# New order for batches 0 to 2 of a planned attention and gated-MLP kernel

## The chip, the cores and the metric

The kernel runs on one core of one Trainium2 chip. A core has TensorE (PE, with the weight load PEld beside it), VectorE (DVE), ScalarE (ACT), GpSimd (POOL) and SyncE (SP), which here only issues DMAs, all in one queue. The metric is the device time of one execution in microseconds (us), as the median of several runs.

## The reference

Eight batches of attention (8 heads, 576 positions, 64 columns a head), whose output is the input of a gated MLP with a product over positions:

```
scores = q @ k.T / 8                     # per batch and head
heads 0-3: keep 0 <= i - j < 32          # local
heads 4-7: keep j <= i, i % 32 == j % 32 # strided
x  = softmax(scores) @ v                 # 8 x 576 x 512
h  = relu(x @ w_in)                      # 512 -> 1024
u, v = h[..., :512], h[..., 512:]
v_n = (v - mean(v)) / sqrt(var(v) + 1e-6)
v_s = w_spatial @ v_n + b_spatial[:, None]   # over the 576 positions
out = (u * v_s) @ w_out                  # 512 -> 512
```

All of it is fp32.

## The kernel before

**Precision.** An fp32 operand of the MLP is split into two parts of a shorter type: `rnd` (L419, recorded at L427 or L429) casts it to the high part, `rest` (L433, recorded at L437) subtracts that from the value to get the low part. Each product then takes three matmuls (high-high, high-low, low-high). So behind every operand of TensorE stand two small operations of ACT, DVE or POOL.

**Stages of a batch b.** Heads are worked in four pairs, t = 4b + hp, hp 0 and 1 local, hp 2 and 3 strided. Local scores are the products L565 and their output L675; strided scores L711 and their output L781; the result is split into x. Then come the value product (L1034, over four 128-wide slabs kt of x), its statistics and normalisation (`chain`, L992 to L1017), which gives vn; the gate product U (L1234); the spatial product (L1331, weights wsp_sb, 48 matmuls for four blocks of 128 columns; the last 64 positions, called the tail, and the bias come in at L1343 and L1344); the gating on DVE (L1354); and the output product (L1435), which is done as seven block products of half size on sums and differences of the blocks of g and of w_out (the sums are `combine`, L902). The w_in, wsp and w_out operands are brought in during the first batch: w_in and w_out come as pairs of words that ACT (L866), POOL or DVE (L875) and DVE (L883) put together, and are split like any operand.

**What sets the order.** Nothing is issued in the order of the code. Each operation is added to a `Program` with a key and with the engines that may do it and their assumed costs. `order` replays the program with those costs, and each engine that comes free takes the ready operation of lowest key. If an operation may run on DVE or POOL, it is given to whichever the replay ends first on, and DVE's end is made later for the comparison by a constant: `dp` holds one for operations with a single input and one for those with two, and they hold while the replay's clock is under `dpt`, else the constant is 0 (L293). The instructions are then written to each engine in this order, loads to SP. `KEYS` holds the keys: `a` for each of the first eight attention tiles, `v`, `u`, `s`, `t`, `o` for the slabs of w_in (value half, gate half), wsp, its tail and w_out, `lq`, `lw`, `lv`, `lu`, `lo`, `ls` for their loads, `cst`, `fill` and `set` for constants and clears, and `p`, `b`, `p2`, `b2`, `cl`, `ta`, `la`, `su`, `tu` for offsets in later stages. `fillers` (L332) puts matmuls on zeros (L1622) ahead of a product where the replay shows a gap: `w` holds until when in the replay, from which gap on, and for which share of it.

Of the kernel before, what the change touches and what calls it, by code (L numbers as in the profile page):

```python
# [39 lines left out]
TAIL = S - 4 * P  # L40
NT = 4
KEYS = {
    "a": (-7906.0, -7964.0, -15830.5, -4267.6, 1379.5, 702.2, 2039.1, -3334.8,),
    "v": (5971.0, -3908.5, -3534.4, 726.2,),
    "u": (4329.4, -8322.8, -3410.6, -6121.6,),
    "s": (13308.3, 1709.1, 5210.5, 13961.2,),
    "t": (2702.5,),
    "o": (1519.5, 3986.0, -8051.8, 12581.5,),
    "cst": (-11921.6,),
    "lead": (-1.3,),  # L50
    "fill": (-7688.6, 5328.4, -10489.4, 9430.7, 11172.9, 3859.6,),
    "dp": (12894.8, -1038.4,),
    "dpt": (657.16,),
    "lv": (-2858.0, -4582.1, -8989.4, -1041.3,),
    "lu": (66.6, -1740.1, -5229.0, 1297.1,),
    "lo": (-7685.9, 12601.4, 4211.2, 6006.6,),
    "ls": (3541.9, 11770.0, 12130.5, 1637.8, 8461.5,),
    "near": (4868.39,),
# [4 lines left out]
    "set": (-100.0, -90.0, -90.0,),  # L63
    "w": (110.0, 0.7, 0.8,),
    "p2": (11.39, 28.77, 1.25,),
    "b2": (-94.81, -0.95, -162.68, -62.31, 5.91, 7.53, 69.31, -30.15, -133.03, -14.06, 0.12,),
    "cl": (-13.99, 175.03, -54.21, -178.21, -336.22, -30.36,),
    "ta": (482.31, 200.01,),
    "la": (8.82, -81.27, -24.66, -78.03,),
    "su": (240.79, 97.41,),  # L70
    "tu": (-0.95, -65.62, 102.01, 7.87, 89.32, -152.34, 100.98, -246.45,),
}
U_COST = 11.2
WARM_COST, WARM_COLS = 427.0, 256
PE_MASKED, APART = (0, 1, 2, 3), (0, 1)
OTHER_BANK = (1, 2, 3)
# [87 lines left out]
class Program:  # L164
# [39 lines left out]
    def order(self):  # L204
# [41 lines left out]
        while len(issued) < len(ops):  # L246
# [14 lines left out]
            now, e = best  # L261
# [28 lines left out]
                cost += FETCH_COST * max(0.0, -stock)  # L290
            now = max(free[e], ready_at[n][e])
            locks = POOL in self.port.get(n, ()) and self.share[n] == 1
            held = KEYS["dp"][locks] if now < KEYS["dpt"][0] * 1000.0 else 0.0  # L293
            other = []
            for o, c in ops[n][1]:
                if o != e:
# [2 lines left out]
            if other and min(other)[0] < now + cost + shared(n, e, now, cost)[0] + held * (e == DVE):  # L299
                e = min(other)[1]  # L300
                cost = dict(ops[n][1])[e]
                now = max(free[e], ready_at[n][e])
            taken[n] = True
            if e in self.port.get(n, ()):
                more, theirs = shared(n, e, now, cost)
                cost += more
                p = peer[e]
# [55 lines left out]
def attention_moe(ctx, tc, qT, kT, ks, vl, vs, cst, eye, w_in, w_out, wsp, wtail, out):  # L363
# [839 lines left out]
    def moe_1(b, key):  # L1203
        if b >= SEVEN:
            moe_u(b, key)
            key += U_COST
        vn = vns[b] = r_vn.new()
# [499 lines left out]
```

## Time and profile before

| what | value |
|---|---|
| median of 3 runs | 516.87 us (516.08 to 517.52) |
| the profiled execution | 518.85 us |
| its span on the core | 517.0 us, 14639 instructions |
| mean granted TensorE clock | 0.979 |
| traffic | 42.27 MB read, 9.44 MB written, 100 GB/s over the span |
| loads, KB each: q, k, kbd, v_raw (local), xt or v_raw (strided) | 295, 304, 144, 384, 512 |
| loads, KB each: one slab of w_in or w_out, cst, eye | 512, 96, 64 |

The span is what the core's trace covers; the execution's own time holds 1.85 us more. In the rows, "x" stands for x0 and x1, "m", "po" and "s" are accumulation tiles, "pts" and "ptl" the transposed attention weights; a row of a timeline is a start, a length, the engine, the line and what is written from what, with the idle time ahead of it and what ended that in brackets.

### The profile page before, as it was taken

What the parts mean: (1) busy time and instruction counts of PE and PEld (TensorE: products, weight loads), DVE (VectorE), ACT (ScalarE), POOL (GpSimd) and SP (SyncE); (2) the same over time, 40 slices, a digit from 0 to 9 for tenths busy, and PEclk for the clock granted to TensorE, in tenths of its full rate; (3) what the DMA queues carried; (4) which work ended last, traced back from release to release, by engine and by line L of the source; (5) the groups of instructions that cost most, each with busy time, mean ns of one, the idle gap of its engine ahead of it and who ended that gap; (6) DMA issues with size and microseconds to landing.
All of it is one profiled execution on the core that took longest, in us unless ns stands there. A gap on an engine that the chain in (4) does not pass through costs nothing.

```text
span 517.0 us, 14639 instructions
## 1 busy us (share of the span) xinstructions
PE 494.2 (96%) x5824; PEld 451.1 (87%) x5824; DVE 407.8 (79%) x1140; ACT 270.9 (52%) x801; POOL 142.3 (28%) x256
## 2 busy tenths in 40 slices
PE   6779979999999999899999999999999998999997
PEld 4558879989899899899899998999899997899897
DVE  2799899969489769998699958997699648784566
ACT  5786765569453685476354646457264414241222
POOL 3455864043222134211131306212120102210200
PEclk9688989999999999999999999999999999999999
DMA  8796522444035413233033603324030300011002
GB/s 273 296 335 231 182 83 81 168 123 135 2 125 159 144 49 115 93 112 109 2 119 113 195 2 94 115 67 129 1 97 20 115 1 2 1 46 47 1 1 93
DMA packets 26244, 52.65 MB, mean 102 GB/s; under 512 B 3136, under 2 KB 11584, under 8 KB 26176
## 3 DMA queue, kind: packets, MB, share of 16 engines
q1 hardware_dynamic: 26176, 51.72, 30.1%
q8 instruction: 46, 0.75, 0.6%
q14 instruction: 22, 0.18, 0.1%
HBM read 42.27 MB, written 9.44 MB: 100 GB/s over the span
## 4 chain that ended last, share of the span: by engine, by line
PE 79%; DVE 10%; DMA 4%; POOL 2%; ACT 2%; issue 1%; SPq 1%; POOLq 0%; DVEq 0%; ACTq 0%
PE m L1034 17%; PE m L1331 17%; PE m L1435 15%; PE m L1157 10%; PE m L1234 5%; PE po L781 4%; PE po L675 3%; PE s L565 2%; PE m L1343 2%; DMA outT<-vv 2%; PE s L711 1%; DVE x L437 1%; DVE vn L437 1%; PE m L1344 1%; DMA k<-kT 1%
## 5 line engine op out<-in xcount | busy, mean ns | idle before, releaser
L1331 PE MATMUL m<-wsp_sb,vn 128*128 128x288 f32 x720 | 106.4, 299 | 5.3 <-DVE wsp_sb L437 3.8
L1331 PEld LDWEIGHTS m<-wsp_sb,vn 128*128 128x128 f32 x720 | 100.1, 191 | 7.4 <-DVE wsp_sb L437 4.1
L1034 PE MATMUL m<-w_in_sb,x 128*128 128x512 f32 (+1 forms) x408 | 100.9, 403 | 0.0
L1034 PEld LDWEIGHTS m<-w_in_sb,x 128*128 128x128 f32 (+1 forms) x408 | 75.5, 188 | 19.4 <-DVE x L437 0.2
L992 ACT ACTIVATE vv<-m 128x512 f32<-128x512 f32 (+1 forms) x37 | 21.8, 596 | 65.8 <-PE m L1034 65.3
L429 POOL TENSOR_SCALAR ptl<-pc 32x320 f32<-32x320 f32 (+3 forms) x86 | 41.5, 483 | 53.1 <-PE po L675 18.8
L1435 PE MATMUL m<-g,w_out_sb 128*128 128x288 f32 x384 | 55.5, 296 | 0.0
L622 ACT ACTIVATE pl<-pl,ml 128x64 f32<-128x64 f32 (+1 forms) x140 | 47.2, 341 | 15.3 <-DVE ml L602 15.1
L1010 POOL TENSOR_TENSOR bn<-bn,sel 128x1 f32<-128x1 f32 (+1 forms) x37 | 21.8, 593 | 115.1 <-DVE bn L1005 114.1
L1435 PEld LDWEIGHTS m<-g,w_out_sb 128*128 128x128 f32 x384 | 52.4, 188 | 0.3 <-DVE o L1463 0.2
L1435 PE MATMUL m<-vn,w_out_sb 128*128 128x288 f32 x288 | 42.1, 297 | 0.0
L997 DVE BATCH_NORM_STATS2 bn<-vv 128x6 f32<-128x512 f32 (+1 forms) x37 | 25.4, 686 | 19.8 <-ACT vv L992 19.5
L429 POOL TENSOR_SCALAR pts<-pc 32x288 f32<-32x288 f32 x37 | 17.5, 472 | 84.8 <-DVE pc L765 59.1
L1234 PE MATMUL m<-x,w_in_sb 128*128 128x288 f32 x288 | 40.2, 297 | 0.0
L1435 PEld LDWEIGHTS m<-vn,w_out_sb 128*128 128x128 f32 x288 | 39.2, 188 | 0.7 <-DVE o L1463 0.2
L427 ACT COPY ptl<-pc 32x64 f32<-32x64 f32 (+3 forms) x106 | 36.4, 345 | 6.0 <-DVE pc L646 3.1
L1234 PEld LDWEIGHTS m<-x,w_in_sb 128*128 128x128 f32 x288 | 38.8, 188 | 0.7
L1017 DVE TENSOR_SCALAR vv<-vv,bn 128x512 f32<-128x512 f32 (+1 forms) x37 | 21.2, 572 | 13.9 <-POOL bn L1010 13.7
L427 ACT CAST g<-u 128x576 fp32r<-128x576 f32 (+1 forms) x33 | 20.0, 610 | 19.2 <-DVE u L1356 12.7
L1168 DVE TENSOR_TENSOR u<-m,vv 128x288 f32<-128x288 f32 x30 | 13.4, 449 | 18.7 <-PE m L1157 18.6
L622 ACT ACTIVATION_READ_ACCUMULATOR pl<-pl,ml 128x1 f32 (+1 forms) x140 | 26.8, 191 | 0.0
L437 DVE TENSOR_TENSOR g<-u,g 128x576 fp32r<-128x576 f32 (+1 forms) x40 | 24.5, 631 | 0.8 <-ACT g L427 0.7
(187 smaller groups left out, 967.1 us busy)
## 6 DMA issues: line engine op xcount, KB each, us to landing
q<-qT SPq DMA_DIRECT2D x30, 295.0 KB, 4.2
outT<-o SPq DMA_DIRECT2D x48, 144.0 KB, 1.8
k<-kT SPq DMA_DIRECT2D x16, 304.0 KB, 4.3
kbd<-ks SPq DMA_DIRECT2D x32, 144.0 KB, 3.6
v_raw<-vl SPq DMA_DIRECT2D x11, 384.0 KB, 5.0
v_raw<-vs SPq DMA_DIRECT2D x8, 512.0 KB, 5.1
xt<-vs SPq DMA_DIRECT2D x7, 512.0 KB, 3.6
outT<-vv SPq DMA_DIRECT2D x16, 144.0 KB, 1.8
```

The costliest lines, as they stand in the source:

```text
L427: eng.copy(dst(), src())
L429: eng.tensor_scalar(dst(), src(), 1.0, 0.0, op0=ALU.mult, op1=ALU.add)
L437: eng.tensor_tensor(dst(), src(), f32(hi()), op=ALU.subtract)
L622: eng.activation(p_sb()[:m, u, :], src, AF.Exp, bias=st()[:m, u : u + 1], scale=SCALE if masked else -1.0, **total,)
L992: lambda eng: eng.activation(v()[:m], v_ps()[:m, :], AF.Relu), [(v_ps,)], [(v,)],
L997: lambda eng: eng.bn_stats(bn()[:m, 0:6], v()[:m]), [(v,)], [(bn,)],
L1010: lambda eng: eng.tensor_tensor(bn()[:m, 9:10], bn()[:m, 8:9], sel[:m, 0:1], op=ALU.pow),
L1034: eng.matmul(v_ps()[:m, :], x_at(kt)[:, a, :], w_in_sb[:, w, kt, HF:], start=(n == 0 and i == 0), stop=(n == NT - 1 and i == 2),)
L1157: eng.matmul(o_ps()[:, :HS], w_at(w)[:, a * P : (a + 1) * P], x_at(j), start=first and kk == 0 and i == 0, stop=kk == 1 and i == 2, skip_g ...
L1234: eng.matmul(u_ps()[:, :HS], w_in_sb[:, w, kt, f * P : (f + 1) * P], xs[NHP * b + kt]()[:, a, r], start=(n == 0 and i == 0), stop=(n == NT ...
L1331: eng.matmul(s_ps()[:, :HS], vn()[:, a, kt, fs], wsp_sb[:, w, kt, r], start=(kt == 0 and i == 0), stop=False,)
L1435: eng.matmul(o_ps()[:, :HS], w_out_sb()[:, b_at, w, kk, a * P : (a + 1) * P], at(j, kk), start=first and kk == 0 and i == 0, stop=kk == 1 ...
```

## The change

New values for nearly all of `KEYS`, and one rule: the engine constants `dp` now hold for the replay's first 115 us, and after that the constants of before (12894.8 and -1038.4) hold to the end, where it was 0 after 657.16. The constants of the first 115 us make DVE dearer for operations with two inputs (436.0, was -1038.4) and less dear for those with one (3807.8, was 12894.8). `w` now asks for a gap of 28.64 us, so no matmul on zeros is left.

```diff
 KEYS = {
-    "a": (-7906.0, -7964.0, -15830.5, -4267.6, 1379.5, 702.2, 2039.1, -3334.8,),
+    "a": (-17466.3, -17745.4, -23530.8, -11905.7, 3036.6, 5737.4, 8267.3, -10389.9,),
...
-    "dp": (12894.8, -1038.4,),
-    "dpt": (657.16,),
+    "dp": (3807.8, 436.0,),
+    "dpt": (115.0,),
...
-    "w": (110.0, 0.7, 0.8,),
+    "w": (150, 28.64, 0.86,),
...
 }
 U_COST = 11.2
+HELD = (12894.8, -1038.4)
...
-            held = KEYS["dp"][locks] if now < KEYS["dpt"][0] * 1000.0 else 0.0
+            held = (KEYS["dp"] if now < KEYS["dpt"][0] * 1000.0 else HELD)[locks]
```

The other keys (`v` to `tu`) get new values in the same way. No operation is added or taken out but the 11 matmuls on zeros. Over the whole program DVE has 1122 instructions where it had 1142, ACT 673 (663), POOL 271 (261); SP issues the same 198 loads and stores. From U of batch 2 on, the order differs only in where single attention tiles and output blocks stand. Lines count one higher from L74 on.

**The start, on PE, up to the first value products.** Before (m is a tile of scores or of the value product, x0_0 the first slab of x), with the matmuls on zeros:

```order
L1622 MATMUL po_0_292<-zeros_67 32x256 x3
L781 MATMUL po_0_292<-pts_71,xt_0_87 64x4x18 x8
L781 MATMUL po_1_304<-pts_71,xt_0_87 64x4x18 x8
L711 MATMUL m_3_136<-kbd_68,w_out_sb_0_84 32x36 x32
L1034 MATMUL m_4_382<-w_in_sb_62,x0_0_328 128x512 x3
L1034 MATMUL m_5_393<-w_in_sb_62,x0_0_328 128x512 x3
L1034 MATMUL m_6_405<-w_in_sb_62,x0_0_328 128x512 x3
L675 MATMUL po_2_414<-ptl_72,v_raw0_0_140 64x96 x6
L675 MATMUL po_3_422<-ptl_72,v_raw0_0_140 64x96 x6
L1034 MATMUL m_7_434<-w_in_sb_62,x0_0_328 128x512 x3
```

The same place now:

```order
L712 MATMUL m_3_129<-kbd_68,w_out_sb_0_95 32x36 x32
L782 MATMUL po_0_366<-pts_71,xt_0_306 64x4x18 x8
L782 MATMUL po_1_375<-pts_71,xt_0_306 64x4x18 x8
L676 MATMUL po_2_404<-ptl_72,v_raw0_0_210 64x96 x6
L676 MATMUL po_3_414<-ptl_72,v_raw0_0_210 64x96 x6
L1035 MATMUL m_4_425<-w_in_sb_62,x0_0_392 128x512 x3
L1035 MATMUL m_5_434<-w_in_sb_62,x0_0_392 128x512 x3
L712 MATMUL s_2_443<-kbd_68,q0_1_388 32x36 x32
L1035 MATMUL m_4_425<-w_in_sb_62,x0_1_422 128x512 x3
L1035 MATMUL m_5_434<-w_in_sb_62,x0_1_422 128x512 x3
```

The value product ran four tiles (m_4 to m_7) slab by slab and now runs two, slab after slab, then the other two. The first local output (L675) and the strided scores of t = 3 (m_3) have moved ahead. On SP 0.30 MB of loads stood ahead of the strided values of t = 2 (xt_0), now 5.47 MB, among them the first slab of w_in and the local q and k.

**The spatial weights, on DVE.** Before, ahead of the tail of batch 0 (the steps on vv_4 and bn_4 make tail_0):

```order
L437 TENSOR_TENSOR w_out_sb_1_822<-g_3_735,w_out_sb_1_822 128x256 x2
L437 TENSOR_TENSOR wsp_sb_63<-x1_0_604,wsp_sb_63 128x576 x2
L437 TENSOR_TENSOR wsp_sb_63<-x1_1_605,wsp_sb_63 128x576
L982 TENSOR_TENSOR wt_b_65<-x1_2_772,wt_b_65 96x576
L997 BN_STATS bn_4_1035<-vv_4_1026 64x6
```

Now, between the first normalised tiles (vv_0, vv_1) and their parts vn:

```order
L1018 TENSOR_SCALAR vv_0_616<-vv_0_616,bn_0_625 128x512
L438 TENSOR_TENSOR wsp_sb_63<-x1_1_551,wsp_sb_63 128x576
L1018 TENSOR_SCALAR vv_1_619<-vv_1_619,bn_1_633 128x512
L438 TENSOR_TENSOR wsp_sb_63<-x1_0_550,wsp_sb_63 128x576
L438 TENSOR_TENSOR vn_1_685<-vv_0_616,vn_1_685 128x512
L438 TENSOR_TENSOR vn_1_685<-vv_1_619,vn_1_685 128x512
```

The rests of wsp_sb have moved from just ahead of the tail to ahead of the first vn.

**The first output product's operands, on POOL.** Before, from the tail's cast (tail_b0) on; g_6 to g_9 and vn_2 hold the parts of the gated blocks:

```order
L429 TENSOR_SCALAR tail_b0_73<-vv_4_1026 64x512
L429 TENSOR_SCALAR w_out_sb_1_822<-g_5_1013 128x256
...
L437 TENSOR_TENSOR w_out_sb_1_822<-g_5_1013,w_out_sb_1_822 128x256
L429 TENSOR_SCALAR g_6_1225<-u_2_725 128x288
L429 TENSOR_SCALAR g_7_1234<-u_2_725 128x288
L429 TENSOR_SCALAR vn_2_1278<-u_2_725 128x288
L429 TENSOR_SCALAR g_9_1415<-u_3_924 128x288 x2
```

Now:

```order
L438 TENSOR_TENSOR w_out_sb_1_673<-g_4_935,w_out_sb_1_673 128x256
L430 TENSOR_SCALAR g_6_1156<-u_2_731 128x288
L430 TENSOR_SCALAR w_out_sb_1_673<-g_5_979 128x256
L438 TENSOR_TENSOR g_6_1156<-u_2_731,g_6_1156 128x288
L903 TENSOR_TENSOR u_2_731<-u_3_853,u_2_731 128x288
L438 TENSOR_TENSOR g_7_1195<-u_2_731,g_7_1195 128x288
L903 TENSOR_TENSOR o_2_1221<-u_3_853,u_2_731 128x288
L903 TENSOR_TENSOR u_2_731<-u_2_731,o_2_1221 128x288
L438 TENSOR_TENSOR vn_2_1213<-o_3_1231,vn_2_1213 128x288
L438 TENSOR_TENSOR g_8_1288<-u_2_731,g_8_1288 128x288
L430 TENSOR_SCALAR g_9_1321<-u_3_853 128x288
L438 TENSOR_TENSOR vn_2_1213<-u_3_853,vn_2_1213 128x288
```

POOL did casts there; it now has five rests and three combinations of that width (and one more rest behind these rows), and five local weight casts that stood between the casts have gone elsewhere.

More of the change, by code (lines that the diff above doesn't have):

```diff
@@ L42 @@
 KEYS = {
-    "a": (-7906.0, -7964.0, -15830.5, -4267.6, 1379.5, 702.2, 2039.1, -3334.8,),
[L44 to L51, printed above, removed]
-    "dp": (12894.8, -1038.4,),
-    "dpt": (657.16,),
[L54 to L58, printed above, removed]
[4 rows of a table removed]
-    "set": (-100.0, -90.0, -90.0,),
-    "w": (110.0, 0.7, 0.8,),
[L65 to L71, printed above, removed]
+    "a": (-17466.3, -17745.4, -23530.8, -11905.7, 3036.6, 5737.4, 8267.3, -10389.9,),
+    "v": (-11047.6, -8344.3, -7497.7, 3252.4,),
+    "u": (3450.0, -22944.2, 589.8, -15405.2,),
+    "s": (713.1, 8774.8, 15438.1, -17937.8,),
+    "t": (-11040.6,),
+    "o": (13283.9, 29031.1, 11569.6, -27487.6,),
+    "cst": (-28292.9,),
+    "lead": (-6.06,),
+    "fill": (-10824.3, -8316.7, -1497.4, -11737.2, 13265.7, 11900.6,),
+    "dp": (3807.8, 436.0,),
+    "dpt": (115.0,),
+    "lv": (-6281.4, -17118.8, -11005.2, -5596.9,),
+    "lu": (-10147.4, 268.4, -28205.8, 5087.6,),
+    "lo": (6453.7, -6904.9, -27580.7, -11041.2,),
+    "ls": (13067.8, 23577.7, 12505.4, 4376.2, 23386.0,),
+    "near": (8261.33,),
[4 rows of a table added]
+    "set": (-2782.8, 4369.5, 22233.8,),
+    "w": (150, 28.64, 0.86,),
+    "p2": (20.51, 33.22, 3.75,),
+    "b2": (-152.57, -3.91, -157.13, -81.52, 4.11, 17.97, 93.53, -113.33, -258.11, -66.93, 37.34,),
+    "cl": (173.92, 211.33, 36.15, -105.5, -250.46, -83.21,),
+    "ta": (405.61, 268.37,),
+    "la": (13.78, -206.75, -69.17, -2.33,),
+    "su": (393.15, 160.75,),
+    "tu": (-22.84, 2.01, 116.28, -0.51, 4.08, -128.79, 109.66, -283.61,),
 }
 U_COST = 11.2
+HELD = (12894.8, -1038.4)
 WARM_COST, WARM_COLS = 427.0, 256
```

8 rows, old and new, of the table KEYS are left out of this document.

## The prediction

> **What bounds the kernel now.** First the page's summary by engine, the clock line of its 40 slices, and the chain of work that ended last.
>
> ```profile
> PE 494.2 (96%) x5824; PEld 451.1 (87%) x5824; DVE 407.8 (79%) x1140; ACT 270.9 (52%) x801; POOL 142.3 (28%) x256
> ...
> PEclk9688989999999999999999999999999999999999
> ...
> PE 79%; DVE 10%; DMA 4%; POOL 2%; ACT 2%; issue 1%; SPq 1%; POOLq 0%; DVEq 0%; ACTq 0%
> ```
>
> PE is busy 494.2 of the 517.0 us, so only two things can shorten this: PE's idle time (22.8 us) and the time in which it is busy at a lowered clock (the digits under 9, all in the first 80 us). I therefore cut the span into stages; the columns are length, busy PE, PEld, DVE, ACT, POOL (with instruction counts), granted clock, DMA share and GB/s.
>
> ```profile
> 0.00:20.00 20.00, 12.79 (x240) 7.21 (x240) 7.44 (x23) 10.25 (x25) 6.97 (x18) 0.77 0.90 321
> 20.00:34.80 14.80, 12.03 (x233) 9.12 (x232) 13.61 (x26) 13.96 (x39) 8.61 (x16) 0.96 0.76 254
> 34.80:46.10 11.30, 10.73 (x128) 8.71 (x129) 10.06 (x21) 6.04 (x13) 5.28 (x6) 0.70 0.71 258
> 46.10:64.40 18.30, 18.29 (x214) 16.39 (x212) 16.82 (x54) 14.36 (x49) 14.14 (x19) 1.00 0.62 215
> 64.40:68.20 3.80, 0.02 (x1) 0.02 (x1) 3.80 (x22) 3.68 (x14) 3.48 (x5) 1.00 0.45 146
> 68.20:76.20 8.00, 8.00 (x49) 7.84 (x51) 7.73 (x15) 4.62 (x17) 5.18 (x6) 0.79 0.21 65
> 76.20:141.60 65.40, 65.40 (x982) 59.26 (x982) 51.64 (x182) 41.62 (x141) 20.99 (x43) 1.00 0.32 101
> 200.00:220.00 20.00, 18.21 (x282) 17.25 (x281) 19.89 (x40) 9.92 (x25) 8.39 (x12) 1.00 0.40 132
> 220.00:517.00 297.00, 290.36 (x2972) 271.32 (x2970) 229.09 (x597) 132.16 (x361) 55.55 (x104) 1.00 0.20 64
> ```
>
> Four places lose time: the start-up to 46.1 us (10.75 us idle, clock 0.70 to 0.96), the hole at 64.4 to 68.2, the slow 8 us behind it, and 1.8 us at 200 to 220, where DVE is busy 19.89 of 20. From 76.2 to 141.6 PE is never idle at full clock: nothing put elsewhere shortens that stretch.
>
> The hole, in the waits, in PE's order of time, and in DVE's:
>
> ```profile
> PE m L1331 <- DVE wsp_sb L437: 3.8, 1, 3.8
> ```
> ```profile
> 64.09 0.29 PE L1331 MATMUL m<-wsp_sb,vn 128*128 128x288 f32 x1
> 68.18 8.00 PE L1331 MATMUL m<-wsp_sb,vn 128*128 128x288 f32 x47 [3.79 <-DVE wsp_sb L437]
> 76.11 1.21 PE L675 MATMUL po<-ptl,v_raw 128*64 128x96 f32 x24
> 77.25 0.78 PE L711 MATMUL s<-kbd,q 128*32 128x36 f32 x64
> ...
> 79.14 1.76 PE L1331 MATMUL m<-wsp_sb,vn 128*128 128x288 f32 x12
> 80.75 0.29 PE L1343 MATMUL m<-wt_h,tail 128*128 128x288 f32 x1
> ...
> 86.58 1.76 PE L1435 MATMUL m<-g,w_out_sb 128*128 128x288 f32 x12
> ```
> ```profile
> 59.34 1.09 DVE L437 TENSOR_TENSOR w_out_sb<-g,w_out_sb 128x256 fp32r<-128x256 f32 x1
> ...
> 63.27 1.11 DVE L437 TENSOR_TENSOR vn<-vv,vn 128x512 fp32r<-128x512 f32 x1
> ...
> 66.04 0.74 DVE L437 TENSOR_TENSOR w_out_sb<-g,w_out_sb 128x256 fp32r<-128x256 f32 x2
> 66.71 2.08 DVE L437 TENSOR_TENSOR wsp_sb<-x,wsp_sb 128x576 fp32r<-128x576 f32 x3
> ...
> 74.32 0.68 DVE L437 TENSOR_TENSOR tail<-vv,tail 64x512 fp32r<-64x512 f32 x1
> ```
>
> PE stands still 3.79 us until DVE has formed the rest parts of the spatial weights, which DVE does last, although the last rest of vn was done by 64.38. The product then takes 8.00 us for 47 matmuls, while 12 at full clock take 1.6 us (from 79.14 to the next row's 80.75; the 1.76 holds the pipeline's end): 47 x 1.60/12 = 6.27, so 1.7 us go to the lowered clock (0.79) behind the hole.
>
> **The change, part by part.** The sum is made against the profiled execution: span 517.0 us, 518.85 with the 1.85 us around it; the median of the runs is 516.87, so I carry the difference over to that.
>
> 1. *Spatial weights formed early.* In DVE's new order these three rests stand ahead of the last rests of vn, more than 40 rows before the tail. The hole's cause is gone: -3.8. If the third and fourth rest of vn, at 64.38 before, come no earlier, PE that reaches the product at 64.1 stops about 1 us on them: bound -2.8. Nothing is behind the moved rests that PE waits for sooner than vn. The three cost 3 x 0.69 = 2.1 us of DVE whether early or late.
>
> 2. *Clock behind the hole.* Without the hole no lowered clock: -1.7 (bound 0 if another hole of like length opens just ahead).
>
> 3. *DVE's work.* These are the groups of DVE and POOL in the first 110 us (busy us, mean ns).
>
> ```profile
> L437 DVE TENSOR_TENSOR w_out_sb<-g,w_out_sb 128x256 fp32r<-128x256 f32 x10 | 5.3, 563 | 0.0
> L437 DVE TENSOR_TENSOR vn<-vv,vn 128x512 fp32r<-128x512 f32 x4 | 3.7, 951 | 0.0
> L437 DVE TENSOR_TENSOR w_in_sb<-vn,w_in_sb 128x512 fp32r<-128x512 f32 x4 | 3.6, 894 | 0.4 <-ACT w_in_sb L427 0.4
> L437 DVE TENSOR_TENSOR g<-u,g 128x288 fp32r<-128x288 f32 x8 | 3.4, 447 | 0.0
> ```
> ```profile
> L437 POOL TENSOR_TENSOR w_out_sb<-g,w_out_sb 128x256 fp32r<-128x256 f32 x4 | 4.4, 1096 | 0.2
> L429 POOL TENSOR_SCALAR g<-u 128x288 fp32r<-128x288 f32 x4 | 2.1, 547 | 6.1 <-DVE g L437 4.4 <-DVE w_out_sb L437 1.7
> L902 POOL TENSOR_TENSOR g<-g,g 128x256 f32<-128x256 f32 x2 | 1.9, 948 | 0.0
> L429 POOL TENSOR_SCALAR vn<-u 128x288 fp32r<-128x288 f32 x1 | 1.9, 1855 | 2.5 <-PE m L1331 2.5
> ```
>
> Eighteen two-input operations go from DVE to POOL, nearly all in batches 0 to 2: 3 rests of w_in (0.89 each, 2.7), 2 of vn from vv (0.95, 1.9), 6 rests of 288 wide (0.45, 2.7), one of w_out (0.56) and 6 combinations of like width (0.45 by the same rows, 2.7). That is 10.6, and some 11.5 us with two attention steps. Summing the durations along each order, the tail's last rest has 60.0 us of DVE work up to it where it had 67.3, and the first gate 60.4 where it had 70.8. Against it stands POOL.
>
> ```profile
> 58.99 1.15 POOL L902 TENSOR_TENSOR g<-g 128x256 f32<-128x256 f32 x1
> ...
> 72.70 1.05 POOL L429 TENSOR_SCALAR tail_b<-vv 64x512 fp32r<-64x512 f32 x1 [0.36 <-DVE vv L1017]
> ```
>
> A rest of w_out beside that combination on POOL took DVE 1.09 us (59.34), and two at 66.04 0.74 together, 0.37 each: +0.72 a piece. If all eighteen cost that, 13 us, and DVE gains nothing. I take half of it, leaving DVE 5 us ahead at the tail.
>
> What this is worth to PE: with the hole gone PE asks for the tail at 64.4 + 6.3 + 1.9 (two attention blocks, the rows at 76.11 and 77.25) = 72.6. At DVE's old pace the tail is there at 75.0, a wait of 2.4 us; with a lead of 5 us at 70, no wait.
>
> [...]
>
> 4. *POOL's chain ahead of the first output product.* Between the tail's low half and the last part of g, POOL had some 7 us of work; now it has 19 operations one behind the other: 8 of 256 or 512 wide (0.45 to 1.1 each by the rows above, 7.4), two casts of 288 at 0.55, and nine two-input ones of 288 that I price at 1.17 (the mean of 0.95 and 1.1, times 288/256): 19.0 us up to the last part, 11.6 up to the second product's. From the tail's cast, which ended at 73.75, moved up by DVE's 5, the second is there at 80.4 and the last at 87.8. PE reaches the output product at 86.6 - 3.8 - 1.7 = 81.1 (term 5 left aside) and runs its seven blocks of 12 matmuls at 1.7 us each, so they are due at 82.8 and 91.3: on the means all of it fits, with 3.5 us to spare at the end. Bounds: 0, and +8 (the only 288-wide operation caught beside a busy DVE took 1.855 us; nine and two at that size end 8.8 later, 5.3 late, and half of DVE's lead lost adds 2.5). I take **+2.0**, nearer to the means, which are most of the rows.
>
> 5. *Start-up.* No warm matmuls on zeros now; keys and first weight slab are loaded ahead of the strided values. In PE's order of time before:
>
> ```profile
> 13.90 1.12 PE L565 MATMUL s<-k,q 64*32 64x64 f32 x59 [1.44 <-DMA k<-kT]
> ...
> 17.43 2.77 PE L1622 MATMUL po<-zeros 128*32 128x256 f32 x6
> ...
> 37.48 4.89 PE L1034 MATMUL m<-w_in_sb,x 128*128 128x512 f32 x12
> 42.30 0.97 PE L565 MATMUL s<-k,q 64*32 64x64 f32 x72
> 43.20 3.06 PE L1034 MATMUL m<-w_in_sb,x 128*128 128x512 f32 x12
> ```
>
> The first key tile now follows 1.90 MB of loads instead of 2.42, the second 2.51 instead of 3.43: at the slice's 321 GB/s 1.6 and 2.9 us earlier. That helps what waits for keys (1.44 us here). But the strided values come after 5.99 MB, not 0.83, the first attention output (x, hp 0) has 17.0 us of DVE work up to it and not 10.9, and the last (hp 3) 29.5 and not 28.7. The last sets the end of the value product. Behind it PE now has 30 matmuls, since it runs two tiles at a time, where it had 12: at full clock (3.06 for 12) 4.6 us more, but the old order lost as much at the lowered clock (4.89 for 12) and in waits. Bounds: -4 (both key gains, no loss), +3 (30 matmuls at the clock of the 4.89 row). I take **-1.0**.
>
> [...]
>
> 6. *Batches 3 to 7* keep PE full except at 200 to 220 and some 6.6 us after. New keys there shift attention pieces and output blocks among each other; the amounts of work are the same. 0, with +-2: one hole like the 1.8 us at 200 to 220, more or less.
>
> Sum: -3.8 - 1.7 + 2.0 - 1.0 + 0 = -4.5: 514.35 for the profiled execution, **512.4 us** for the median.
>
> **Rivals.**
> *POOL becomes the bound (slower).* It decides once the nine two-input operations average over 1.17 + 3.5/9 = 1.56 us: at worst term 4 is then +8, and a hole of that length costs the 1.7 of lowered clock again: -4.5 - 2.0 + 8 + 1.7 = +3.2, 520.1. For it: POOL works the 19 off one by one, and DVE is busy 7.73 of 8.00 us at 68.2 to 76.2; against: POOL is busy only 20.99 of 65.40 us there before.
> *The gain is eaten.* DVE's lead is nil (2.4 us of wait at the tail) and the start-up goes to +1: -3.8 - 1.7 + 2.4 + 1 = -2.1, 514.8.
> *Cold start.* Without the warm block the clock stays low until the value product is through: its last 30 matmuls take 12.2 us (4.89 for 12), not 7.6, term 5 is +3 and the time 516.4. For it: 0.77 and 0.70 in the slices there; against: the clock was back at 0.96 between them without any matmul on zeros after 20.2.
> *Swallowed later.* DVE, 19.89 of 20 busy at 200 to 220, sets the pace later, so what PE gains before 76 us it waits for there. Against: DVE has 11 us less to do by then. 516.9.
> *More.* DVE's 10.4 us at the first gate and both key gains reach PE: -3.8 - 1.7 - 4 = -9.5, 507.4.
> That the change doesn't do what it says is excluded: both orders show the moves.
>
> **Numbers.** Forecast (gain of 2.5 to 7.5) 0.50; more than that 0.09; eaten (gain of 1.6 to 2.5) 0.07; cold start and swallowed later 0.07 each; POOL, or another cause of a loss, 0.20. Within 0.3%, 1.6 us, a measurement here can't tell a change from none. So faster 0.66, same 0.14, slower 0.20. The likeliest case's own range is 509.4 to 514.4; to leave out no more than 2 in 10, I take 506.0 to 518.5, which drops the worst of POOL's case.
>
> **What would show it.** Right: no wait of the spatial product on wsp_sb, clock 1.00 in that product, value product over before 46 us, first gate some 5 us earlier. Wrong: a wait of the output product (L1435, now L1436) on POOL's parts of g or vn; DVE's rests at twice their length; a clock near 0.5 through the value product; a larger hole at 200 to 220.

## The result

The change runs in 520.91 us (median of 4, 520.17 to 521.36) against 516.71 for the kernel before in the same series: 1.0079 times as long, 95% interval 1.006 to 1.0098. Forecast was 512.4, so the sign was wrong, and 520.91 lies outside the range of 506.0 to 518.5. In later series the kernel before had medians of 517.35 to 518.29, so below each kernel is given with its ratio to the kernel before in its own series.

The page of the change, by engine, and its clock line:

```profile
span 518.8 us, 14591 instructions
...
PE 487.5 (94%) x5802; PEld 448.6 (86%) x5802; DVE 408.5 (79%) x1120; ACT 273.6 (53%) x811; POOL 157.2 (30%) x266
...
PEclk9999999999999999999999999999999999999999
```

PE is less busy than before (487.5 us for 494.2, of which the matmuls on zeros were 7.9), but the span is longer: its idle time rose from 22.8 to 31.3 us. Most of that rise lies in the first 20 us (7.2 to 13.6), where the matmuls on zeros had counted as busy. By the same stages as before (length, busy PE, PEld, DVE, ACT, POOL, clock, DMA share, GB/s):

```profile
0.00:20.00 20.00, 6.37 (x218) 5.53 (x218) 9.35 (x25) 12.39 (x35) 7.72 (x19) 1.00 0.86 311
20.00:34.80 14.80, 12.83 (x225) 10.60 (x226) 12.34 (x27) 11.85 (x30) 13.37 (x19) 1.00 0.74 251
...
64.40:68.20 3.80, 3.80 (x31) 3.80 (x30) 1.44 (x4) 3.44 (x9) 2.42 (x6) 1.00 0.60 219
68.20:76.20 8.00, 5.75 (x122) 5.15 (x121) 6.51 (x18) 4.12 (x10) 5.17 (x6) 1.00 0.11 21
76.20:141.60 65.40, 64.27 (x976) 57.56 (x974) 52.92 (x193) 44.13 (x163) 31.86 (x55) 1.00 0.36 109
```

The hole at 64.4 to 68.2 is gone, as forecast. In its place stand 2.25 us at 68.2 to 76.2, and 1.1 us in a stretch where PE was never idle. PE's order of time shows where:

```profile
20.90 1.45 PE L712 MATMUL m<-kbd,w_out_sb 128*32 128x36 f32 x64 [8.08 <-DMA kbd<-ks]
...
27.66 2.59 PE L1035 MATMUL m<-w_in_sb,x 128*128 128x512 f32 x6
...
43.47 3.05 PE L1235 MATMUL m<-x,w_in_sb 128*128 128x288 f32 x20
46.82 0.79 PE L1235 MATMUL m<-x,w_in_sb 128*128 128x288 f32 x4 [0.30 <-DVE w_in_sb L438]
...
49.61 1.22 PE L782 MATMUL po<-pts,v_raw 128*64 128x72 f32 x32 [1.09 <-DMA v_raw<-vs]
...
63.23 6.52 PE L1332 MATMUL m<-wsp_sb,vn 128*128 128x288 f32 x48
71.99 0.41 PE L1344 MATMUL m<-wt_h,tail 128*128 128x288 f32 x1 [2.25 <-DVE tail L438]
...
82.85 1.76 PE L1436 MATMUL m<-g,w_out_sb 128*128 128x288 f32 x12
...
85.71 1.06 PE L1436 MATMUL m<-g,w_out_sb 128*128 128x288 f32 x6 [0.40 <-ACT vv L450]
...
240.42 1.05 PE L1158 MATMUL m<-x,w_in_sb 128*128 128x288 f32 x6 [0.96 <-ACT vv L450]
...
333.27 0.40 PE L1344 MATMUL m<-wt_h,tail 128*128 128x288 f32 x1 [1.10 <-DVE tail L438]
```

The reader sees the spatial product run through at full clock (48 in 6.52 us where 47 took 8.00), PE reach the first output product at 82.85 instead of 86.58, and then small waits, new or longer than before (of these kinds the kernel before has 0.4 us for a tail and 0.3 for a read-out between 40 and 350 us). One more thing: the clock line says 9 everywhere, yet six matmuls at 27.66 take 2.59 us, 0.43 each, where 12 of them take 2.80 at full clock, 0.23 each. The clock was low there. The trace's first record of the clock begins only at 29.70 us, and the views count time without a record as full clock; five of these six matmuls start ahead of it. So at the start of a trace the pitch of equal matmuls (the time from the start of one to the start of the next) is the better clock.

**A ruler for both.** Orders differ, so equal places in the trace are not equal amounts of work. I give each matmul its shortest usual pitch (0.2335 us for a value matmul, 0.1335 for a 288 wide one, 0.0475, 0.036, 0.0125 and 0.011 for L675, L781, L565 and L711 by the lines of before), sum this along PE's order to a work of 469.9 us, the same for every kernel here, and subtract it from the time at which it is reached. What is left is time lost so far, by idling or by a low clock. All numbers are us; the execution of each trace is named in the head.

| work done (stage) | before, second trace (517.9) | before without zeros (515.2) | the change (520.6) | best kernel below (515.7) |
|---|---|---|---|---|
| 10 | 18.5 | 19.3 | 23.4 | 22.7 |
| 20 (value product ends) | 24.9 | 21.7 | 23.7 | 23.2 |
| 30 (in U) | 25.3 | 23.7 | 25.8 | 24.9 |
| 40 (first spatial product) | 30.3 | 26.9 | 25.7 | 24.9 |
| 50 (second half of it) | 31.2 | 28.6 | 28.5 | 26.4 |
| 70 (first output product done) | 31.7 | 29.1 | 31.0 | 28.1 |
| 110 | 32.6 | 30.0 | 31.9 | 28.9 |
| 180 | 35.9 | 33.3 | 35.5 | 33.7 |
| 300 | 37.9 | 35.1 | 40.1 | 35.5 |
| end | 42.6 | 39.7 | 44.9 | 40.3 |

Against the kernel before, the change is 0.5 behind in U, 4.6 ahead at work 40, 2.7 at 50, 0.7 at 70, and 2.3 behind at the end. That is less than the 4.2 us between the medians; both traced executions of the kernel before (518.85, 517.9) were above its first median, so part of the 4.2 is not in a trace.

### The profile page after: what moved, and what is told of

Read it like the earlier page. It is cut to its first block, busy times and chain, and to the rows that moved or that the text cites. A ratio compares the mean times of both kernels' runs of the same rounds, so it can differ in the third digit from the quotient of the medians.

```text
span 518.8 us, 14591 instructions
## 1 busy us (share of the span) xinstructions
PE 487.5 (94%) x5802; PEld 448.6 (86%) x5802; DVE 408.5 (79%) x1120; ACT 273.6 (53%) x811; POOL 157.2 (30%) x266
## 3 DMA queue, kind: packets, MB, share of 16 engines
q1 hardware_dynamic: 26176, 51.72, 30.3%
## 4 chain that ended last, share of the span: by engine, by line
PE 64%; DVE 17%; DMA 7%; POOL 6%; issue 3%; ACT 2%; SPq 1%; ACTq 0%; POOLq 0%; DVEq 0%
PE m L1035 15%; PE m L1332 13%; PE m L1436 12%; PE m L1158 9%; PE m L1235 5%; DVE vn L438 3%; DMA outT<-vv 2%; PE po L676 2%; PE po L782 2%; PE s L566 2%; DMA vn<-w_in 2%; DMA g<-w_out 2%; DVE x L438 2%; POOL ptl L430 1%; DMA k<-kT 1%
## 5 line engine op out<-in xcount | busy, mean ns | idle before, releaser
L1332 PE MATMUL m<-wsp_sb,vn 128*128 128x288 f32 x720 | 104.7, 296 | 1.6 <-DVE u L1355 1.4
L1332 PEld LDWEIGHTS m<-wsp_sb,vn 128*128 128x128 f32 x720 | 98.5, 189 | 3.8 <-DVE u L1355 1.6
L1035 PE MATMUL m<-w_in_sb,x 128*128 128x512 f32 (+1 forms) x408 | 99.4, 399 | 0.0
L1011 POOL TENSOR_TENSOR bn<-bn,sel 128x1 f32<-128x1 f32 (+1 forms) x37 | 22.8, 618 | 129.8 <-DVE bn L1006 129.5
L430 POOL TENSOR_SCALAR ptl<-pc 32x320 f32<-32x320 f32 (+3 forms) x82 | 37.0, 451 | 43.2 <-DVE pc L647 17.4
L428 ACT COPY ptl<-pc 32x320 f32<-32x320 f32 (+3 forms) x110 | 38.1, 348 | 9.2 <-DVE pc L647 7.5
L1169 DVE TENSOR_TENSOR u<-m,vv 128x288 f32<-128x288 f32 x30 | 13.6, 453 | 14.7 <-PE m L1158 12.6
```

The lines of the kernel that those rows point to most:

```text
L428: eng.copy(dst(), src())
L430: eng.tensor_scalar(dst(), src(), 1.0, 0.0, op0=ALU.mult, op1=ALU.add)
L1011: lambda eng: eng.tensor_tensor(bn()[:m, 9:10], bn()[:m, 8:9], sel[:m, 0:1], op=ALU.pow),
L1035: eng.matmul(v_ps()[:m, :], x_at(kt)[:, a, :], w_in_sb[:, w, kt, HF:], start=(n == 0 and i == 0), stop=(n == NT - 1 and i == 2),)
L1332: eng.matmul(s_ps()[:, :HS], vn()[:, a, kt, fs], wsp_sb[:, w, kt, r], start=(kt == 0 and i == 0), stop=False,)
```

## The experiments

### The matmuls on zeros, and the two sets of keys

The first series had four kernels: the kernel before again; the change with the later keys of before; the kernel before with the later keys of the change; and the kernel before without matmuls on zeros.

```diff
 # before_nowarm: the kernel before
-    "w": (110.0, 0.7, 0.8,),
+    "w": (150, 28.64, 0.86,),
 # after_oldlate: the change, p2 b2 cl ta la su tu as before; before_newlate: the reverse
-    "p2": (20.51, 33.22, 3.75,),
+    "p2": (11.39, 28.77, 1.25,),
...
-    "tu": (-22.84, 2.01, 116.28, -0.51, 4.08, -128.79, 109.66, -283.61,),
+    "tu": (-0.95, -65.62, 102.01, 7.87, 89.32, -152.34, 100.98, -246.45,),
```

> The kernel before, unchanged, for a second trace: its first trace belongs to an execution of 518.85 us, 2.1 above the median of the others. Theory A (that trace caught an unlucky clock at the start): span near 515.0, with less lowered clock in the first 76 us, 2 us less lost there, and the change then loses some 4 us against it in the first 220 us or later. Theory B (tracing itself costs 2 us, spread over the span): span near 517.0 again, the losses by stage those of the first trace.

> The change with the later keys (p2, b2, cl, ta, la, su, tu) as before; the order up to U of batch 2 or 3 is the change's own. Theory A (the later keys lose the 2.3 us that the change loses between 220 and 340 us): 518.5 us. Theory B (the loss is made in batches 0 to 2, the later keys are neutral): 520.9, within 1.

> The kernel before with the change's later keys alone (p2, b2, cl, ta, la, su, tu); its first 140 us are as before. Theory A (the later keys lose): 519.0 us, with 2.3 us more idle PE between 220 and 340. Theory B (they are neutral): 516.7, within 1.

> The kernel before without its 11 matmuls on zeros, all else the same. Theory A (they keep the clock up through the first products in most executions): 2 to 4 us slower, 518.7 to 520.7, first products at half clock. Theory B (the clock falls before the value product anyway, as in the first trace): 516.7, within 1.

Measured: the second trace of the kernel before belongs to 517.9 us, 0.3 above the median of its series (517.61), with 42.6 us lost where the first had 43.6. Neither 515.0 nor 517.0 of span came out (516.1): the trace was a little unlucky, no more.

Without matmuls on zeros the kernel before takes **515.36 us, ratio 0.9959 (0.9941 to 0.9977)**: neither theory, the cold start works the other way round. The windows of the two show where (same columns as above; the second trace of before first, then without zeros).

```profile
20.00:25.00 5.00, 4.70 (x112) 3.76 (x110) 4.24 (x10) 4.29 (x14) 3.05 (x7) 0.96 0.52 175
...
35.00:40.00 5.00, 5.00 (x39) 4.28 (x40) 5.00 (x11) 2.31 (x6) 1.40 (x3) 0.50 1.01 398
```
```profile
20.00:25.00 5.00, 4.74 (x73) 3.89 (x73) 4.34 (x11) 4.83 (x14) 2.34 (x6) 0.50 0.51 144
...
35.00:40.00 5.00, 5.00 (x108) 3.96 (x104) 5.00 (x10) 2.77 (x6) 1.09 (x2) 1.00 1.01 389
```

With zeros the clock was up at 20 to 25, where PE works small attention products, and down at 35 to 40, where the long value product runs. Without them it is the other way round, and 3.2 us less are lost at work 20 (24.9 to 21.7). The two other traces of these kernels bear this out: the first with the zeros has the clock at half from 34.72 to 41.54 us, 6.8 us, and the second without them a clock of 0.83 at 30 to 40 us, 3.4 us at half. The zeros did not hold the clock; with them it was up sooner and low again where that cost more.

The later keys exchanged: the change with the old ones 525.71 us (ratio 1.014, 1.0098 to 1.0181), the kernel before with the new ones 526.1 (1.0153, 1.0121 to 1.0184). Both theories fall: each set is worse on the other's first half, by 4.8 us (3.2 by the ratios) and 8.5. In the second, one wait alone is 4.9 us, of PE's local scores on a load of q. A key is only worth something beside the replay in which it was set, so a change of keys does not cut an effect out. From there on I therefore also wrote the issue order out, and moved single operations in it.

### Parts of the change alone, by keys

```diff
 # nowarm_wsp_early: the kernel before without zeros
-    "s": (13308.3, 1709.1, 5210.5, 13961.2,),
+    "s": (-3308.3, -1709.1, -5210.5, -3961.2,),
 # nowarm_newrule: the kernel before without zeros, dp, dpt and the held line of the change
-    "dp": (12894.8, -1038.4,),
-    "dpt": (657.16,),
+    "dp": (3807.8, 436.0,),
+    "dpt": (115.0,),
 # after_warm: the change
-    "w": (150, 28.64, 0.86,),
+    "w": (110.0, 0.7, 0.8,),
 # after_oldrule: the change
-    "dp": (3807.8, 436.0,),
-    "dpt": (115.0,),
+    "dp": (12894.8, -1038.4,),
+    "dpt": (657.16,),
```

> The kernel before without matmuls on zeros and with the keys of the spatial weights alone moved (s), so that their rests stand ahead of the last rests of vn on DVE; from about 140 us on the order is that of before. Compared with the kernel before without matmuls on zeros (515.36 us). Theory A (the hole ahead of the first spatial product goes, a wait of some 2.4 us for the tail comes): 3 us faster, 512.4. Theory B (DVE has the same work before the first gate, so the whole of it moves to the tail and the gates): 515.4, within 1.

> The kernel before without matmuls on zeros and with the change's engine rule (dp, dpt, HELD), its own keys. Against 515.36 us: theory A (the rule puts two-input operations on POOL, whose chain makes the first output product wait 2 us, as in the change): 517.4 or more. Theory B (DVE's relief is worth more): 513 or less.

> The change with the rule for matmuls on zeros as before (three rows of them come back, all else the same). Theory A (they only shift the stretch of lowered clock into the value product, as the kernel before shows against its copy without them): 2 us slower than the change, 523. Theory B (the change's start is long idle, from 13 to 21 us, and loses by the missing matmuls): 2 to 4 us faster, 517 to 519.

> The change with the engine constants as before (dp, dpt): 18 operations come back from POOL to DVE in batches 0 to 2. Theory A (the chain on POOL and the casts on ACT behind it cost 2 us at the first output product): 519, no wait of that product on ACT. Theory B (DVE, with them back, is late at the tail and the gates): 521 or more, with a wait for the tail of over 4 us.

Measured: 520.75 us (1.0067, 1.0041 to 1.0092) with wsp early, 537.18 (1.0378) with the new rule on the old keys, 521.18 (1.0078, 1.0054 to 1.0103) for the change with zeros back, 526.95 (1.0188) for the change with the old rule.

The rule is worth 6 us in the change and costs 22 on the old keys: again a pair. Theory B gave the sign for the change with the old rule, but not its reason: PE's wait for the first tail there is 2.2 us, not over 4. What the 22 us consist of was not followed. The zeros make no difference that can be told in the change (521.18 for 520.91), so neither theory holds there. The first kernel teaches most: its rests stand where they were asked to, and it lost 5 us against its base of 515.36, which neither theory had. DVE and PE there:

```profile
57.83 1.82 DVE L437 TENSOR_TENSOR wsp_sb<-x,wsp_sb 128x576 fp32r<-128x576 f32 x2 [1.72 <-POOL wsp_sb L429]
...
69.32 0.69 DVE L997 BATCH_NORM_STATS2 bn<-vv 64x6 f32<-64x512 f32 x1 [1.61 <-ACT vv L992]
```
```profile
67.40 3.79 PE L1331 MATMUL m<-wsp_sb,vn 128*128 128x288 f32 x24 [0.68 <-ACT u L1248]
74.97 0.61 PE L1343 MATMUL m<-wt_h,tail 128*128 128x288 f32 x1 [3.78 <-DVE tail L437]
```

The rests now stand ahead of vn in DVE's queue, but their casts on POOL, which had waited for the load of wsp, are not done, and DVE stands idle 1.72 us for them, and later 1.61 us more for ACT's read-out of the tail. The tail is there at 74.97, PE waits 3.78 us for it, and the clock is 0.50 at 75 to 80 us. The row moved ahead of its data did not wait alone; all that stood behind it on DVE waited with it. The change had moved the loads of wsp forward as well: the last two are issued at 50.92 here, in the change two at 38.49 and the last at 49.42.

### The order written out: splices and single moves

These kernels take the keys of their base, but the order is a list of operations with their engines. The instructions of each engine come out the same as the base's where nothing is moved.

```diff
     def emit(self, nc, warm):
-        issued = self.order()
-        fillers = self.fillers(issued)
-        for _, n, e in issued:
-            if e == PE and fillers.get(n):
-                warm(self.spare[n][1], fillers[n])
-            self.ops[n][2](getattr(nc, e))
+        engine = {e[0]: e for e in ENGINES} | {"a": ACT, "v": DVE, "g": POOL, "s": DMA, "t": PE}
+        for word in WRITTEN.split():
+            self.ops[int(word[1:])][2](getattr(nc, engine[word[0]]))
 # after_lateold: WRITTEN is the change's order up to 127 us of its replay, then that of before
 # nowarm_lateafter: the reverse
 # after_tail_first, on the rows of ACT (POOL and DVE alike for the tail's other steps):
+L993 ACTIVATE vv_4<-m
 L428 COPY ptl<-pc_5  x7
-L993 ACTIVATE vv_4<-m
 # nowarm_swap, on the rows of ACT and DVE:
+L427 CAST wsp_sb<-x
 L427 COPY ptl<-pc_5  x7
-L427 CAST wsp_sb<-x
 L437 vn_1<-vv_3
+L437 wsp_sb<-x x3
 L437 w_out_sb<-g
...
 L437 w_out_sb<-g x2
-L437 wsp_sb<-x x3
```

> The change up to 127 us of the replay, and from there the order and engines of the kernel before, word for word; at that point both have done the same operations. Theory A (some 3 us of the loss lie in the change's own late order): 517.3, no more than 9.8 us lost after the splice. Theory B (the late loss follows from the state in which the change arrives): 520.9, within 1.

> The reverse: the kernel before without matmuls on zeros up to 127 us of the replay, and from there the change's order and engines. Against 515.4 us: theory A (the change's late order loses 3 us wherever it starts): 518.6. Theory B: 515.4, within 1.

> The change with one chain moved ahead in the queues: ACT reads the tail's value product out before seven casts of ptl instead of behind them, POOL does the tail's power ahead of one L876, DVE and ACT the tail's steps ahead of one w_out piece; nothing else moves. Theory A (the 2.25 us wait for the tail is the place of a casual row in ACT's queue and is simply lost): 518.7. Theory B (DVE and POOL hold the gates and the first output product anyway): 520.9, within 1, the wait found again in the output product.

> The kernel before without matmuls on zeros, in which four rows alone move: ACT's cast of the last slab of wsp ahead of its casts of ptl, and DVE's three rests of wsp to just behind the last rest of vn, ahead of 16 rows of attention and three rests of w_out. Theory A (of the 3.0 us hole and the lowered clock behind it 3 us go): 512.4, a wait of at most 1.5 us, clock 1.00 behind it. Theory B (DVE has as much to do before the tail and the gates as ever, the wait moves there): 515.4, within 1.

**The late order.** 517.30 us (0.9991, 0.9976 to 1.0005) and 518.91 (1.0029, 1.0013 to 1.0044): 3.6 us better than the change (4.5 by the ratios), and 3.5 worse than the base (3.6 by the ratios), as theory A has it. In the traces the time lost from work 110 to the end is 13.0 in the change (44.9 - 31.9) and 12.9 in the reverse splice (43.7 - 30.8), 9.7 in the base and 10.2 in the splice. So the change's late order loses some 3 us wherever it starts. PE's waits between 140 and 340 us name two pieces of it, here in the reverse splice:

```profile
PE m L1343 <- DVE tail L437: 1.5, 2, 1.1
PE m L1331 <- DVE u L1354: 1.4, 1, 1.4
PE m L1157 <- ACT vv L449: 0.8, 1, 0.8
```

and in the splice with the order of before:

```profile
PE m L1332 <- DVE u L1355: 1.4, 1, 1.4
PE m L1344 <- DVE tail L438: 0.4, 1, 0.4
```

The wait for the gated u is in both; 1.1 us more for a later tail and 0.8 of the U product for a tile that ACT has still to read out are the late order's own. That is 1.9 of the 3; the rest is in waits under 0.3 us and was not followed further.

**The tail.** 517.94 us (1.0013, 0.9997 to 1.0029), 3.0 better than the change (3.4 by the ratios), as theory A has it and more. The rows of ACT, in the change and then with the move:

```profile
64.64 2.57 ACT L428 COPY ptl<-pc 32x320 f32<-32x320 f32 x7 [2.41 <-DVE pc L647]
67.24 0.59 ACT L993 ACTIVATE vv<-m 64x512 f32<-64x512 f32 x1
```
```profile
61.83 0.59 ACT L993 ACTIVATE vv<-m 64x512 f32<-64x512 f32 x1 [0.72 <-PE m L1035]
63.73 2.57 ACT L428 COPY ptl<-pc 32x320 f32<-32x320 f32 x7 [1.31 <-DVE pc L647]
```

and DVE's next step on the tail in the change:

```profile
67.86 0.69 DVE L998 BATCH_NORM_STATS2 bn<-vv 64x6 f32<-64x512 f32 x1 [2.36 <-ACT vv L993]
```

In the change ACT stood idle for 2.41 us, with the tail's product waiting in its queue behind seven casts whose input DVE had not made. Moved ahead, the tail costs the casts nothing. PE's wait falls from 2.25 to 1.04 us:

```profile
69.17 0.40 PE L1344 MATMUL m<-wt_h,tail 128*128 128x288 f32 x1 [1.04 <-DVE tail L438]
```

That is the 1.2 us which the traces show for the move (2.7 lost from work 40 to 50, then 1.5). The trace as a whole is better by 3.3, but 1.6 of that lie ahead of the move (24.2 lost at work 30 for 25.8), which it cannot have caused. So the medians say 3.0, and the traces do not show where more than 1.2 of it comes from.

**Three rests of wsp on the old order.** 516.84 us (0.9987, 0.9973 to 1.0002): not better than its base (0.9959 and, below, 0.9950). PE's rows:

```profile
62.43 8.00 PE L1331 MATMUL m<-wsp_sb,vn 128*128 128x288 f32 x47 [1.93 <-DVE wsp_sb L437]
...
75.37 1.86 PE L1331 MATMUL m<-wsp_sb,vn 128*128 128x288 f32 x12 [1.81 <-DVE u L1354]
```

The hole is 1.93 us where the base's two traces have 2.98 and 4.01, and a new wait of 1.81 us stands behind it, for the gates on DVE. Theory B, or a little worse: what fills the hole on DVE is work that has to be done before the gates in any case. (The trace is of the fastest of its twelve executions, 514.73.) The clock falls behind the hole all the same (0.77 at 65 to 70 us, 47 matmuls in 8.00 us).

### Together, contention, loads

```diff
 # after_tail_late: the change with the moves of after_tail_first and the splice of after_lateold
 # after_tail_late_dve: the same, nine operations ahead of the first output product
-POOL L438 g_6, g_7, g_8, g_9, vn_2 (x2), L903 u_2 (x2), o_2
+DVE  L438 g_6, g_7, g_8, g_9, vn_2 (x2), L903 u_2 (x2), o_2
 # after_kbd_early: the change, on the rows of SP
+L458 q, kbd x2 (t = 3), xt_0<-vs
 L458 vn_0<-w_in, u_0<-w_in, g_1<-w_in
-L458 q, kbd x2 (t = 3), xt_0<-vs
```

> The change with both edits that have been measured alone: the tail's chain ahead in the queues of ACT, POOL and DVE (3.0 us faster alone), and the order of the kernel before from 127 us of the replay (3.6 us faster alone). Theory A (two separate losses that add up): 514.3, faster than the kernel before by 3. Theory B (one loss seen twice, DVE behind PE at both places): 517, within 1.

> The same, and the nine two-input operations of 288 wide ahead of the first output product go from POOL back to DVE, at the same places in the order. Theory A (on POOL each costs DVE 0.6 us by contention, 1.05 against 0.45, more than the 0.45 that it saves): 0.5 to 2 us faster than without that, the first output product without a wait on ACT. Theory B (DVE is full there, 5.0 us of 5; the nine take 4 us of it): 1 to 3 us slower.

> The change with four loads moved in SP's queue: q and the keys of t = 3 and the strided values of t = 2 go ahead of three slabs of w_in. Theory A (PE's 8.1 us wait for these keys is lost time): 518, V starting 3 us earlier. Theory B (the value product ends when the last slab of w_in and of x are there, and these 1.1 MB only move the wait): 520.9, within 1.5.

> The kernel before without matmuls on zeros, once more (its order written out as a list, the instructions the same), since the copy of it with wsp moved came out at 516.84 in another series. Theory A (the gain of 2.2 us over the kernel before is steady): 515.4, 0.4% under the kernel before. Theory B (it was that series' luck): 516.5 or more, then the moved rests of wsp were worth nothing or a little.

Measured: **515.07 us (0.9939, 0.992 to 0.9959)** with both edits. Alone they moved the ratio from 1.0079 by 0.0088 and 0.0066; the sum is 0.9925, within the interval. They are separate losses.

With the nine operations back on DVE: **514.13 us (0.9916, 0.9894 to 0.9937)**. The step of 0.9 us over the kernel without it is within the spread of both, so the times alone do not show it; the traces have 0.9 us less lost from work 50 to 70 (2.6, then 1.7), and the groups of DVE at 74 to 92 us show how, with the nine on POOL and then on DVE (busy us, mean ns):

```profile
L438 DVE TENSOR_TENSOR g<-u,g 128x288 fp32r<-128x288 f32 x4 | 3.2, 798 | 0.3 <-POOL g L430 0.3
...
L903 DVE TENSOR_TENSOR o<-u,u 128x288 f32<-128x288 f32 x1 | 1.0, 1044 | 0.0
```
```profile
L438 DVE TENSOR_TENSOR g<-u,g 128x288 fp32r<-128x288 f32 x8 | 3.6, 484 | 0.3 <-POOL g L430 0.3
...
L903 DVE TENSOR_TENSOR o<-u,u 128x288 f32<-128x288 f32 x2 | 0.9, 444 | 0.0
```

Four rests of g on DVE took 3.2 us beside POOL's, and eight take 3.6 with POOL out of the way: POOL's four bought 0.4 us. The waits of PE on ACT and on vn in that product, 0.8 us together, are gone. An operation of 0.44 us (o<-u,u) that takes 1.04 beside one of POOL's pays 0.60, nearer to the whole price of 0.72 that the prediction had read off than to the half that it took; the four rests pay 0.31 each on the mean (0.80 for 0.48), nearer to the half.

The loads: 524.15 us (1.0098, 1.0079 to 1.0118), no better than the change (1.0079), perhaps worse. PE's rows:

```profile
16.20 1.44 PE L712 MATMUL m<-kbd,w_out_sb 128*32 128x36 f32 x64 [3.01 <-DMA kbd<-ks]
17.56 2.19 PE L782 MATMUL po<-pts,xt 128*64 128x72 f32 x32
28.31 2.03 PE L676 MATMUL po<-ptl,v_raw 128*64 128x96 f32 x22 [8.56 <-POOL w_in_sb L430]
```

The wait for the keys falls from 8.08 to 3.01 us, and 8.56 us come behind it: the value product waits for its weights. Theory B in kind, though its time was 3 us off (1 by the ratios): what the queue of loads brings first is not what PE waits for last.

Without zeros, again: 516.14 us, ratio 0.9950 (0.9934 to 0.9966). The gain over the kernel before is steady, and the best kernel here is 2 us below that one in the same series (514.13 to 516.14), and 4.2 below the kernel before.

## Why the prediction was wrong

By its own terms, with what the change's trace lost against the second trace of the kernel before (by the table of time lost):

| term | forecast | measured (work from, to) |
|---|---|---|
| 1 and 2, wsp early, clock behind the hole | -5.5 | -5.1 (30 to 40) |
| 3, DVE ahead, no wait for the tail | 0 | +1.9 (40 to 50) |
| 4, POOL at the first output product | +2.0 | +2.0 (50 to 70) |
| 5, start-up | -1.0 | +0.5 (0 to 30) |
| 6, batches 3 to 7 | 0 | +3.0 (70 to the end) |
| sum | -4.5 | +2.3 |

All the signs that the prediction named for being right came: no wait on wsp_sb, full clock in the spatial product, the value product over before 46 us, and the first gate earlier (72.57 us for 78.53 in the first trace). Of the signs of being wrong one came, DVE's rests at nearly twice their length (0.80 us for 0.45, ahead of the output product). Most of the time was lost where no sign had been set: at the tail, and behind 220 us.

**Terms 1 and 2 were right**, in mechanism and size.

**Term 4 was right in size, but not in its mechanism; the size was in part luck.** The nine operations took POOL 0.94 us on average, not 1.17, and PE never waited for a part that POOL had made. It waited 0.62 us for ACT, 0.16 for a part of vn and 0.27 for an output, both made by DVE. ACT's rows show how POOL is behind the first of these:

```profile
84.92 0.43 ACT L428 CAST vn<-o 128x288 fp32r<-128x288 f32 x1 [1.36 <-POOL o L903]
85.26 0.39 ACT L450 COPY vv<-m 128x288 f32<-128x288 f32 x1
```

The read-out that frees PE's tile stands in ACT's queue behind a cast that waits 1.36 us for POOL's combination. And what the nine cost beside that is DVE's time, since its own operations took longer next to POOL's (four rests of g 0.80 us each, and 0.48 with the nine on DVE). With them back on DVE the loss falls only from 2.6 to 1.7 us, so less than half of the 2.0 hangs on them.

**Term 3 failed in its step from DVE to the tail.** DVE's work up to the tail's last rest was shorter, as summed. But the tail was not late by DVE's work: DVE idled 2.36 us ahead of the tail's statistics, for ACT, whose queue held the tail behind seven casts. I had summed the work of one engine ahead of a row and not asked, at each row, whose queue stands behind it. The wait of 2.4 us that I had put in the eaten rival came (2.25), for a reason that I had not named. Moving the row took 1.2 us of that wait away.

**Term 5 put the loss of the zeros at nothing and left out what U would wait for.** The rival of a cold start held that the loss of the zeros would cost. Alone, their loss is a gain of 2.2 us on the kernel before, in two series. In the table the start is 0.5 worse all the same. That much does not stand clear of the spread: the change and the four kernels that keep its start have 24.2 to 25.9 us lost at work 30, the kernel before 25.3 and 25.9. Clear of it is the distance to the kernels without zeros, which have 22.0 to 23.7 there in four traces: the change's own order of loads and products costs what the loss of the zeros gave. The value product did end earlier, as forecast, at 43.5 us for 46.1 in the first trace, and only its first five matmuls ran slow (0.43 us each, later ones 0.23). But what that gave was lost in U, which waits 0.3 us for a weight, and in a wait of 1.1 us for strided values (PE po L782 on the load of v_raw). (The start-up's idle time before, by the lines shown, is 10.55 us, not 10.75; nothing hangs on it.)

**Term 6 was the largest miss.** I priced it at nothing, since the amounts of work are the same and pieces are only shifted among each other. The splices show some 3 us there, whatever the first half. Pieces that are shifted among each other is what the terms ahead of it were made of; there I had looked at each place and here at none. It had needed the same reading of the order at each product whose operands come from another engine: the tails, and U behind a tile still to be read out.

That the forecast lay 8.7 us away (-4.5 against +4.2) is, by these numbers, 1.5 at the start, 0.4 in the hole, 1.9 at the tail and 3.0 late, together 6.8; the other 1.9 lies between the traces (2.3 in lost time) and the medians (4.2), and is not explained by a trace.

## What to carry to other kernels

When an order is rewritten, a stall that goes away is only the first half of the reading: walk on from it, queue by queue, to the next row that PE needs, and ask at each queue whether a row stands behind another that waits (here the tail, 2.41 us behind seven casts on ACT). Two-input operations moved from DVE to POOL bought next to nothing while both were busy (four rests of g 0.4 us); count their length on both. And keys of a planner work as a set: to cut out an effect, edit the order that comes out, not the numbers that go in, since exchanging a part of the numbers that set the order cost 5 to 22 us here, while single rows moved in the written order cost or gave some 3 at most.

## What was not expected of the hardware

- Matmuls on zeros at the start cost the kernel before 2.2 us (the change, nothing that can be told). With them the clock of that kernel was up sooner (by 20 to 21 us in its two traces, without them by 23 to 26 in two), but low again in the long product (0.50 at 35 to 40 us). In the second trace without them a part of a low stretch fell on that product too (12 matmuls in 4.06 us, where 2.80 is full clock), so its place was not the same in the two executions.
- In the first trace of the kernel before, the recorded clock changed only at multiples of 3.41 us from its first record (at 4.00 us): down to half at 10.82, 34.72, 68.85 and 516.00 us, back to full at 21.06, 41.54 and 72.26. Cut into such periods, PE's rows have 2.23 to 2.74 us idle in the four ahead of a fall and 0.00 in the three ahead of a return; the three others at half clock had 0.65 to 2.01 us idle, and no period at full clock with 1.48 us or less was followed by a fall. In the change, recorded from 29.70 us on, the one fall, at 517.81, follows a period with 2.85 us idle; the others have 1.47 at most. So in these traces an idle time of a like length had the clock fall behind it or not: it fell behind one of 1.93 us in the kernel with three rests of wsp moved, and was full behind the one of 2.25 us in the change (the tail's matmuls from 72.24 on follow each other at 0.13 to 0.14 us), of which 0.92 lay in one period and 1.33 in the next. What makes the clock fall is not shown by this.
- A two-input operation of DVE (o<-u,u, 128x288) took 1.04 us beside one of POOL and 0.44 without. In five such cases of 128x288 in the change, DVE's operation started 0.71 to 0.74 us before POOL's ended and ended 0.31 to 0.32 us behind it.
